# A fused attention and two-layer kernel: three of four key casts on ScalarE instead of two, and the written-out order of the program recomputed

## The chip, the core and the metric

The kernel runs on one core of a Trainium2 chip. A core has engines that each work through a program of their own, in order: TensorE (PE, with its weight loads listed as PEld), VectorE (DVE), ScalarE (ACT), GpSimd (POOL), and SyncE (SP), which issues transfers. The metric is device time in microseconds (us) of one execution, as the median over repeated executions.

## The reference

The inputs are q, k and v of shape (4, 8, 768, 64) (batch, heads, positions, head size), one decay number per head, and two weight matrices, 512x2048 and 2048x512.

```python
# per head, in blocks of 64 positions
intra = (q_b @ k_b.T) * Dmask          # lam^(i-j) on and below the diagonal, 0 above
out_b = intra @ v_b + (q_b * lam_pow) @ kv_state
kv_state = lam**64 * kv_state + (k_b * rev_pow).T @ v_b
# then, on x = all heads side by side, 3072 x 512
h = x @ w_in
g = where(h >= 1, h, where(h <= -1, 0, (h + 1)**2 / 4))
return g @ w_out                        # 3072 x 512, float32
```

## The kernel before, in words

**Tiles.** The 3072 positions are cut into 24 chunks of 128 (C), six to a batch. Attention goes chunk by chunk; four chunks make one of six tiles of 512 positions (MS), on which the two weight layers run. Matrix products take bfloat16 and add up in float32. The decay is put into tables: q is multiplied by a table of lam powers, v by its inverse, so that the mask that is left is only the triangle of ones (`causal`).

**Attention of a chunk.** Chunks 0 to 3 (PLAIN) go a different way, with transposes on PE. Chunks 4 to 23 go as follows, and these are the ones that the change touches. k, q and v of the chunk arrive by three transfers of 256 KB (tiles x1f, x0f and x2f). k is cast to bfloat16 in four pieces, each for half of the partitions and every second head (`f_ki`, lines 259 to 264); the list `KE` says for each piece whether ACT (line 262) or DVE (line 264) does it. The pieces and the scaled q (`f_qn`, line 267, DVE) go to one tile kq, of which there are three. SP then issues one transposing transfer of kq into the tile xq (line 273). POOL scales and casts v in four pieces (line 281) and copies them in two (line 284). PE multiplies k and v into the state pu (line 312), ACT casts the state to ubd (line 315), PE multiplies xq with xq into the scores ps (line 324), DVE multiplies these with the triangle into sc (line 331, "the mask product"), and PE multiplies state and scores into po (lines 349 and 351). ACT casts po to the tile xT (line 358).

**The two layers.** PE multiplies xT with w_in into ph (line 368); there are two ph buffers. ACT takes each to r with a relu and a bias of 1 (line 376). For each two r, DVE makes t (line 382), w (line 386) and gT (line 401), which together are the function g. PE multiplies gT with w_out into py (line 407), ACT copies py to osb (line 412), and SP sends it out (line 416). We call a *block* either one filling of ph (16 matmuls of 128 columns, or 8 of 256) or four matmuls into py. There are 96 of each kind, 192 in all.

**What sets the order.** The order of every engine's program is written out when the program is built. Each operation is entered with `add`: a name, an engine, an assumed length in ns, the operations it needs, and a due time. `run_plan` goes through an imagined time with these lengths; whenever an engine is free it takes, of the operations that are ready, the one due first. What comes out is only the sequence of each engine; on the chip each engine follows its sequence and waits for what it needs. So another assumed length can change the sequence anywhere behind it, on all engines. Where the imagined PE would be idle early on, `run_plan` puts in matmuls on zeros (line 232), and their number follows from the imagined times too. The due time of a piece of k or q is 16000 ns ahead of that of the chunk's po (`due=od - 16000`).

Of the kernel before, what the change touches and what calls it, by code (L numbers as in the profile page):

```python
# [15 lines left out]
def _bc(ap, idx, n):  # L16

    a = list(ap.ap)
    a = a[:idx] + [[0, n]] + a[idx:]
    return bass.AP(ap.tensor, ap.offset, a)  # L20
# [3 lines left out]
def kernel(  # L24
# [29 lines left out]
    CPS = MS // C  # L54

    PLAIN, KA = 4, 1
    LD, RING, VBN, VCN = 6, 6, 620, 600
    KE = ('ACT', 'DVE', 'ACT', 'DVE')
    RW, NR = 2, 3
    DBG = False  # L60

# [2 lines left out]
    ld = ctx.enter_context(tc.tile_pool(name="ld", bufs=LD))  # L64
# [81 lines left out]
    def tabq(i, hp):  # L146
        r = row[:, i * C:(i + 2) * C].rearrange("p (a b) -> p a b", b=C)
        nc.scalar.activation(out=tab_q[:, i:i + 2, hp, :], in_=r, func=AF.Exp, scale=ln_t[:, hp:hp + 1])
# [26 lines left out]
    def add(key, eng, ns, fn, needs=(), due=None, extra=0):  # L175
        OPS[key] = Op(key, eng, ns, fn, needs, due, extra)
        ops.append(OPS[key])
# [60 lines left out]
    def mm(*cols):  # L238
        return sum(c / 2.4 + 3 for c in cols)
# [9 lines left out]
    def cast(c, x, e):  # L249
        t = (ks, qs)[1 - x][c] = qkp.tile([128, H, D], BF16, name=f"c{x}", tag=f"c{x}")  # L250
        if e == "ACT":
            nc.scalar.copy(out=t, in_=qkv_ld[c, x])
        else:
            nc.vector.tensor_tensor(t, qkv_ld[c, x], qkv_ld[c, x], op=AX.max)

    def quarter(t, g, hi):
        return t[HD[g]].rearrange("p (a b) d -> p a b d", b=2)[:, :, hi, :]

    def f_ki(c, g, hi):
        o, i = kq[c % NKQ][HD[hi], HP * g:HP * g + HP, HD[hi]], quarter(qkv_ld[c, 1], g, hi)  # L260
        if KE[2 * g + hi] == "ACT":
            nc.scalar.copy(out=o, in_=i)  # L262
        else:
            nc.vector.tensor_tensor(o, i, i, op=AX.max)  # L264

    def f_qn(c):
        nc.vector.tensor_tensor(kq[c % NKQ][:, 2 * HP:, :].rearrange("p a (b d) -> p (a b) d", b=2), qkv_ld[c, 0],  # L267
                                _bc(tab_n[:, c % NCB, :], 2, D), op=AX.mult)
# [6 lines left out]
    def cast_v(c, g=None, hi=None):  # L275
        tab = tab_k[:, c % NCB, :]
        if c < PLAIN:
            nc.gpsimd.tensor_tensor(vn[c % NV], qkv_ld[c, 2], _bc(tab, 2, D), op=AX.mult)
        else:
            tab = tab[HD[g]].rearrange("p (a b) -> p a b", b=2)[:, :, hi]  # L280
            nc.gpsimd.tensor_tensor(vn[c % NV][HD[hi], HP * g:HP * g + HP, :], quarter(qkv_ld[c, 2], g, hi), _bc(tab, 2, D), op=AX.mult)  # L281

    def f_vb(c, hi):
        nc.gpsimd.tensor_copy(vi[c % NV][HD[hi], :, HD[hi]], vn[c % NV][HD[hi]])  # L284

    def f_t(c):
        ptt[c] = pp_t.tile([128, 2, HP, 128], BF16, name="pt", tag="pt")
        for i, x in enumerate((ks, qs)):
            for hp in range(HP):
                nc.tensor.transpose(out=ptt[c][:, i, hp, :], in_=pair(x[c], hp), identity=ident)  # L290

    def f_kb(c):
        kT[c] = ktp.tile([128, HP, 128], BF16, name="kT", tag="kT")
        (nc.scalar.copy if c < KA else nc.vector.tensor_copy)(out=kT[c], in_=ptt[c][:, 0])

    def f_qT(c):
        qT[c] = qtp.tile([128, HP, 128], BF16, name="qT", tag="qT")
        nc.vector.tensor_tensor(qT[c], ptt[c][:, 1], tab_q[:, c % NCB], op=AX.mult)
# [141 lines left out]
    def o_due(c):  # L440
        s, i = c // CPS, c % CPS
        w = CPS // PARTS[s]
        return l_due[1, s, 0, i // w] - LEAD - (w - 1 - i % w) * 8 * STEP
# [46 lines left out]
    for c in range(NCH):  # L490
        od, cb = o_due(c), c % NCB
        P = c < PLAIN
        lu = ("u", c - 1, 1) if cb else ("u", c - 2, 1) if c < PLAIN + 1 else ("u", c - 1, 0)
        lub = [("ub", lu[1], lu[2], hi) for hi in range(2)]
        for x in (1, 0) if P else ():
            e = "DVE" if c == 0 else "ACT"
            add(("cast", c, x), e, 690 if e == "DVE" else 615, lambda c=c, x=x, e=e: cast(c, x, e),
                [("ld", c, x), ("t", c - 3), ("u", c - 3, 1), ("cast", c - 1, x)])
        for hp in range(HP) if P and c % 2 == 0 else ():
            add(("tab", c, hp), "ACT", 410, lambda c=c, hp=hp: tabq(c, hp), [("tab", c, hp - 1), (None, ("kb", 0), ("x", 1))[c // 2]])  # L500
        free = [("xt", c - NKQ), ("u", c - NKQ, 0), ("u", c - NKQ, 1), ("zk", c % NKQ)]
        if not P:
            for g in range(2):
                for hi in range(2):
                    add(("ki", c, g, hi), KE[2 * g + hi], 375, lambda c=c, g=g, hi=hi: f_ki(c, g, hi), [("ld", c, 1)] + free, due=od - 16000)
            add(("qn", c), "DVE", 690, lambda c=c: f_qn(c), [("ld", c, 0), ("tabn",)] + free, due=od - 16000)
        fv = [("ld", c, 2), ("tabk",), ("o", c - NV), ("u", c - NV, 0), ("u", c - NV, 1), ("vb", c - NV, 0), ("vb", c - NV, 1)]
        if P:
            add(("cast", c, 2), "POOL", 1060, lambda c=c: cast_v(c), fv + [("cast", c - 1, 2)], due=-1)
        for g in range(0 if P else 2):  # L510
            for hi in range(2):
                add(("cv", c, g, hi), "POOL", VCN, lambda c=c, g=g, hi=hi: cast_v(c, g, hi), fv + [("cv", c - 1, g, hi)], due=-1)
        for hi in range(0 if P else 2):
            add(("vb", c, hi), "POOL", VBN, lambda c=c, hi=hi: f_vb(c, hi), [("cv", c, 0, hi), ("cv", c, 1, hi), ("o", c - NV), ("zv", c % NV)], due=0)
        if P:
            add(("t", c), "PE", mm(*[128] * 8), lambda c=c: f_t(c), [("cast", c, 0), ("cast", c, 1), ("kb", c - 1), ("qT", c - 1)], due=od - 9000, extra=FILL)
            add(("kb", c), "ACT" if c < KA else "DVE", 590 if c < KA else 430, lambda c=c: f_kb(c), [("t", c), ("s", c - 2, 1)])
            add(("qT", c), "DVE", 690, lambda c=c: f_qT(c), [("t", c), ("o", c - 3), ("qT", c - 1)] + [("tab", c // 2 * 2, hp) for hp in range(HP) if c < NCB])
        else:
            add(("xt", c), "SP", 1800, lambda c=c: f_xt(c), [("ki", c, 0, 0), ("ki", c, 0, 1), ("ki", c, 1, 0), ("ki", c, 1, 1), ("qn", c), ("s", c - NXT, 1), ("o", c - NXT)], due=-0.7, extra=4700)  # L520
        for j in range(1 if P else 0, 2):
            if (cb, j) == (NCB - 1, 1):
                continue
            add(("u", c, j), "PE", mm(*[128 if c < NCB else 64] * 4), lambda c=c, j=j: f_u(c, j),
                [("cast", c, 1), ("cast", c, 2), *(("ki", c, j, hi) for hi in range(2)), *(("cv", c, j, hi) for hi in range(2)), *([("vb", c, 0), ("vb", c, 1)] if c < NCB else []),
                 *([lu] + lub if j == 0 or P else [("u", c, 0), ("ub", c, 0, 0), ("ub", c, 0, 1)])], due=od - 6000 + 1500 * j, extra=FILL)
            for hi in range(2):
                add(("ub", c, j, hi), "ACT", 372, lambda c=c, j=j, hi=hi: f_ub(c, j, hi), [("u", c, j), ("o", (2 * c + j - NUB + 1) // 2)])
        for h in range(0 if P else 1, 2):
            add(("s", c, h), "PE", mm(*[128] * 4) if P else mm(*[64] * 8), lambda c=c, h=h: f_s(c, h),  # L530
                [("kb", c), ("qT", c), ("xt", c), ("m", c, 0) if h and P else ("m", c - 1, 1)],
                due=od - 5500 + 2000 * h, extra=FILL)
            add(("m", c, h), "DVE", 690, lambda c=c, h=h: f_m(c, h), [("s", c, h), ("o", c - 2), ("m", c, 0) if h else None])
        ub = [("ub", c - 1, 1, hi) for hi in range(2) if cb] + [("ub", c, 0, hi) for hi in range(0 if P else 2)]
        add(("o", c), "PE", mm(*[128] * (4 if cb else 0), *[128] * 4) if P else mm(*[64] * (16 if cb else 12)), lambda c=c: f_o(c),
            [("m", c, 1), ("vb", c, 0), ("vb", c, 1), *ub, ("x", c - 1), ("o", c - 1)], due=od, extra=FILL)
        add(("x", c), "ACT", 600, lambda c=c: f_x(c), [("o", c), ("x", c - 1), ("l1", (c // CPS - 2) * FO + FO - 1)])

    n_of = {x: n for n, x in enumerate(l1_order)}
    for n1, (s, i, p) in enumerate(l1_order):  # L540
# [4 lines left out]
            due=l_due[1, s, i, p], extra=FILL)  # L545
# [47 lines left out]
```

## Time and profile before

| | |
|---|---|
| median of 13 executions | 228.55 us (226.49 to 231.53) |
| the profiled execution's own time | 227.48 us |
| its span on the core | 225.3 us |
| clock granted to PE | full throughout |
| busy: PE, DVE, ACT, POOL | 207.7, 175.4, 141.9, 126.7 us |

The profile is of one execution. Its span is 2.2 us shorter than that execution's time, and that execution is 1.07 us under the median. "Busy" is time in which an engine has an instruction running; waits are given with the instruction that ended them. In lists of instructions a row reads: line, engine, operation, tile written <- tiles read, shapes, count, then busy us and mean ns, then idle time of the engine just before.

### The profile page before, as it was taken

The numbers are of one execution on the slowest core, as the hardware profiler recorded it, in microseconds if no ns is written. First come the engines' busy times: TensorE is split into PE (matmuls) and PEld (weight loads), VectorE is DVE, ScalarE is ACT, GpSimd is POOL, SyncE is SP. The second block draws the span as 40 slices with busy tenths as digits, with TensorE's granted clock in tenths as the row PEclk, the third lists the DMA queues.
The fourth block names the chain that finished last, engine by engine and source line by source line (L and its number), as shares of the span: only waits on it lengthen the run. The fifth ranks groups of instructions, "written<-read, shape, count | busy, mean of one in ns | idle before, by whom it ended". The sixth has DMA issues, their size and how long they took to land.

```text
span 225.3 us, 5683 instructions
## 1 busy us (share of the span) xinstructions
PE 207.7 (92%) x2312; PEld 146.9 (65%) x2312; DVE 175.4 (78%) x257; ACT 141.9 (63%) x286; POOL 126.7 (56%) x160
## 2 busy tenths in 40 slices
PE   7799999799799996799997989996999999999993
PEld 3457897466487685587865867765677776766441
DVE  6535899999989999999999799799989555454300
ACT  6757565486396784669756876875568664555121
POOL 8989964599799997926576547556826000000000
PEclk9999999999999999999999999999999999999999
DMA  5999999999999998299987589699374521110212
GB/s 139 220 249 258 258 207 175 254 231 268 272 248 205 258 209 198 67 226 199 204 209 164 137 171 232 152 170 220 90 169 118 54 65 47 49 47 7 89 50 89
DMA packets 98729, 37.59 MB, mean 167 GB/s; under 512 B 90512, under 2 KB 94608, under 8 KB 98704
## 3 DMA queue, kind: packets, MB, share of 16 engines
q1 hardware_dynamic: 93056, 28.84, 58.7%
q0 software_dynamic: 5504, 8.39, 17.4%
q8 instruction: 18, 0.29, 0.6%
q14 instruction: 7, 0.06, 0.1%
q10 hardware_dynamic: 144, 0.00, 0.0%
HBM read 27.27 MB, written 6.29 MB: 149 GB/s over the span
## 4 chain that ended last, share of the span: by engine, by line
PE 52%; DVE 33%; DMA 5%; issue 4%; POOL 3%; ACT 1%; ACTq 0%; POOLq 0%
PE py L407 23%; PE ph L368 23%; DVE kq L264 8%; DVE w L386 7%; DVE t L382 5%; DVE gT L401 5%; DVE kq L267 4%; DVE sc L331 4%; DMA w_in_sb<-in_moe_w_in_dram 3%; DMA x2f<-in_v_dram 2%; PE po L351 2%; PE pu L312 1%; PE po L349 1%; POOL x2f L450 1%; PE ps L324 1%
## 5 line engine op out<-in xcount | busy, mean ns | idle before, releaser
L368 PE MATMUL ph<-xT,w_in_sb 128*128 128x128 bf16 (+1 forms) x1152 | 98.8, 237 | 0.4 <-DMA w_in_sb<-in_moe_w_in_dram 0.4
L407 PE MATMUL py<-w_out_sb,gT 128*128 128x512 bf16 x384 | 94.0, 379 | 0.0
L376 ACT ACTIVATE r<-ph,one 128x512 bf16<-128x512 f32 x96 | 65.5, 687 | 41.4 <-PE ph L368 31.4
L368 PEld LDWEIGHTS <-w_in_sb 128*128 128x128 bf16 x1152 | 80.8, 98 | 13.4 <-DMA w_in_sb<-in_moe_w_in_dram 0.7
L281 POOL TENSOR_TENSOR vn<-x2f,tab_k 64x256 bf16<-64x256 f32 x80 | 65.2, 814 | 42.4 <-DMA x2f<-in_v_dram 34.7
L407 PEld LDWEIGHTS <-gT 128*128 128x128 bf16 x384 | 35.0, 98 | 29.7
L382 DVE TENSOR_SCALAR t<-r 128x1024 bf16<-128x1024 bf16 x48 | 27.2, 567 | 18.0 <-ACT r L376 17.8
L401 DVE TENSOR_TENSOR gT<-w,t 128x1024 bf16<-128x1024 bf16 x48 | 39.8, 829 | 1.5
L386 DVE TENSOR_TENSOR w<-r,t 128x1024 bf16<-128x1024 bf16 x48 | 39.4, 821 | 1.3
L284 POOL COPY vi<-vn 64x512 bf16<-64x512 bf16 x40 | 33.7, 842 | 2.1
L315 ACT CAST ubd<-pu 64x256 bf16<-64x256 f32 x80 | 29.1, 364 | 5.9 <-PE po L349 3.3
L264 DVE TENSOR_TENSOR kq<-x1f 64x256 bf16<-64x256 f32 x40 | 27.2, 680 | 1.0
L358 ACT CAST xT<-po 128x512 bf16<-128x512 f32 x24 | 14.0, 585 | 15.0 <-PE po L351 12.7
L412 ACT COPY osb<-py 128x512 f32<-128x512 f32 x24 | 14.0, 584 | 14.0 <-PE py L407 12.6
L351 PE MATMUL po<-sc,vi 128*128 128x64 bf16 x160 | 11.7, 193 | 10.8 <-DVE sc L331 10.8
L349 PEld LDWEIGHTS <-ubd 128*128 128x128 bf16 x148 | 10.1, 98 | 13.3 <-issue 11.7
L267 DVE TENSOR_TENSOR kq<-x0f,tab_n 128x512 bf16<-128x512 f32 x20 | 18.0, 902 | 0.3
L262 ACT CAST kq<-x1f 64x256 bf16<-64x256 f32 x40 | 16.1, 402 | 0.4
L331 DVE TENSOR_TENSOR sc<-ps,causal 128x512 bf16<-128x512 f32 x20 | 13.7, 685 | 2.1 <-PE ps L324 1.9
L232 PE MATMUL py<-idle 128*128 128x512 bf16 x40 | 12.2, 438 | 1.2 <-DVE one L119 1.2
L349 PE MATMUL po<-xq,ubd 128*128 128x64 bf16 x148 | 12.6, 193 | 0.0
L351 PEld LDWEIGHTS <-vi 128*128 128x128 bf16 x160 | 10.4, 98 | 1.8
(57 smaller groups left out, 110.0 us busy)
## 6 DMA issues: line engine op xcount, KB each, us to landing
out_dram<-osb SPq DMA_DIRECT2D x24, 256.0 KB, 2.5
x1f<-in_k_dram SPq DMA_DIRECT2D x19, 256.0 KB, 3.9
x0f<-in_q_dram SPq DMA_DIRECT2D x19, 256.0 KB, 4.3
x2f<-in_v_dram SPq DMA_DIRECT2D x18, 256.0 KB, 4.1
w_in_sb<-in_moe_w_in_dram POOLq DMA_DIRECT2D x4, 512.0 KB, 8.7
w_out_sb<-in_moe_w_out_dram POOLq DMA_DIRECT2D x4, 512.0 KB, 9.8
x2f<-in_v_dram POOLq DMA_DIRECT2D x6, 256.0 KB, 6.2
x1f<-in_k_dram POOLq DMA_DIRECT2D x5, 256.0 KB, 7.8
```

What stands on the lines that cost most here:

```text
L264: nc.vector.tensor_tensor(o, i, i, op=AX.max)
L267: nc.vector.tensor_tensor(kq[c % NKQ][:, 2 * HP:, :].rearrange("p a (b d) -> p (a b) d", b=2), qkv_ld[c, 0], _bc(tab_n[:, c % NCB, :], 2, ...
L281: nc.gpsimd.tensor_tensor(vn[c % NV][HD[hi], HP * g:HP * g + HP, :], quarter(qkv_ld[c, 2], g, hi), _bc(tab, 2, D), op=AX.mult)
L284: nc.gpsimd.tensor_copy(vi[c % NV][HD[hi], :, HD[hi]], vn[c % NV][HD[hi]])
L315: nc.scalar.copy(out=ubd[(2 * c + j) % NUB][HD[hi], :, HD[hi]], in_=pu[0][HD[hi], :, HD[hi] if c < NCB else HD[0]])
L351: nc.tensor.matmul(po[:, hp, HD[j]], lhsT=vi[c % NV][:, HP * j + hp, :], rhs=sc_sb[c, 1][:, hp, HD[j]], start=(cb == 0 and j == 0), stop=True)
L368: nc.tensor.matmul(ph[:, j * m:(j + 1) * m], lhsT=w_in_sb[:, ko, (i + j) * 128:(i + j + 1) * 128], rhs=xT[s][:, ko, p * m:(p + 1) * m], st ...
L376: nc.scalar.activation(out=r_t[grp][:, i, :], in_=ph_t[s, ni, part], func=AF.Relu, bias=one[:, 0:1])
L382: nc.vector.tensor_scalar(t_t[grp], r_t[grp], 0.5, 1.0, op0=AX.mult, op1=AX.min)
L386: nc.vector.tensor_tensor(w_t[grp], r_t[grp], t_t[grp], op=AX.subtract)
L401: nc.vector.tensor_tensor(o, w, t, op=AX.mult)
L407: nc.tensor.matmul(py_t[s, ms], lhsT=gT[s][:, ko, ms * 128:(ms + 1) * 128], rhs=w_out_sb[:, ko, :], start=(ko == 0), stop=(ko == FO - 1))
```

## The change: three pieces of k on ScalarE, and other assumed lengths

```diff
-    LD, RING, VBN, VCN = 6, 6, 620, 600
-    KE = ('ACT', 'DVE', 'ACT', 'DVE')
+    LD, RING, VBN, VCN = 6, 6, 740, 730
+    KE = ('ACT', 'ACT', 'ACT', 'DVE')
...
-                    add(("ki", c, g, hi), KE[2 * g + hi], 375, lambda c=c, g=g, hi=hi: f_ki(c, g, hi), [("ld", c, 1)] + free, due=od - 16000)
-            add(("qn", c), "DVE", 690, lambda c=c: f_qn(c), [("ld", c, 0), ("tabn",)] + free, due=od - 16000)
+                    add(("ki", c, g, hi), KE[2 * g + hi], 401 if KE[2 * g + hi] == "ACT" else 540, lambda c=c, g=g, hi=hi: f_ki(c, g, hi), [("ld", c, 1)] + free, due=od - 16000)
+            add(("qn", c), "DVE", 750, lambda c=c: f_qn(c), [("ld", c, 0), ("tabn",)] + free, due=od - 16000)
```

The second piece of each of the 20 chunks 4 to 23 goes from line 264 to line 262. Five assumed lengths change: the pieces of k (375 to 401 on ACT and 540 on DVE), the scaled q (690 to 750), and POOL's two kinds of work on v (600 to 730 and 620 to 740). The operations are otherwise the same, except that PE's program has 42 matmuls on zeros instead of 40: where one stood just behind the po of chunk 3, three stand now. The sequences differ on all engines from there on. Three places:

DVE, ahead of the first mask product by the triangle `causal` (chunk 4). kq_128 is the kq tile that chunk 5 uses. Before:

```order
L386 TENSOR_TENSOR w_845<-r,t_843 128x1024
L264 TENSOR_TENSOR kq_128<-x1f 64x4x64 x2
L401 TENSOR_TENSOR gT<-w_845,t_843 128x8x128
L331 TENSOR_TENSOR sc<-ps,causal 128x512
L267 TENSOR_TENSOR kq_128<-x0f,tab_n 128x512
L382 TENSOR_SCALAR t_907<-r 128x1024
```

Now:

```order
L386 TENSOR_TENSOR w_849<-r,t_829 128x1024
L264 TENSOR_TENSOR kq_128<-x1f 64x4x64
L401 TENSOR_TENSOR gT<-w_849,t_829 128x8x128
L267 TENSOR_TENSOR kq_128<-x0f,tab_n 128x512
L331 TENSOR_TENSOR sc<-ps,causal 128x512
L382 TENSOR_SCALAR t_891<-r 128x1024
```

One piece of k is gone from ahead of the mask product, and the scaled q of chunk 5 has come ahead of it.

DVE, around the mask product of chunk 9; kq_128, kq_126 and kq_127 belong to chunks 11, 12 and 13 here. Before:

```order
L267 TENSOR_TENSOR kq_128<-x0f,tab_n 128x512
L382 TENSOR_SCALAR t_1608<-r 128x1024
L386 TENSOR_TENSOR w_1634<-r,t_1608 128x1024
L401 TENSOR_TENSOR gT<-w_1634,t_1608 128x8x128
L264 TENSOR_TENSOR kq_126<-x1f 64x4x64 x2
L267 TENSOR_TENSOR kq_126<-x0f,tab_n 128x512
L331 TENSOR_TENSOR sc<-ps,causal 128x512
L382 TENSOR_SCALAR t_1712<-r 128x1024
L386 TENSOR_TENSOR w_1717<-r,t_1712 128x1024
L401 TENSOR_TENSOR gT<-w_1717,t_1712 128x8x128
L264 TENSOR_TENSOR kq_127<-x1f 64x4x64 x2
```

Now:

```order
L267 TENSOR_TENSOR kq_128<-x0f,tab_n 128x512
L382 TENSOR_SCALAR t_1551<-r 128x1024
L386 TENSOR_TENSOR w_1564<-r,t_1551 128x1024
L401 TENSOR_TENSOR gT<-w_1564,t_1551 128x8x128
L382 TENSOR_SCALAR t_1629<-r 128x1024
L264 TENSOR_TENSOR kq_126<-x1f 64x4x64
L267 TENSOR_TENSOR kq_126<-x0f,tab_n 128x512
L331 TENSOR_TENSOR sc<-ps,causal 128x512
L386 TENSOR_TENSOR w_1692<-r,t_1629 128x1024
L401 TENSOR_TENSOR gT<-w_1692,t_1629 128x8x128
L264 TENSOR_TENSOR kq_127<-x1f 64x4x64
```

Ahead of the mask product one piece of k is gone and the next pair's t has come in its place.

ACT, at the pieces of k of chunks 6 and 7 (kq_126 and kq_127). Before:

```order
L262 CAST kq_126<-x1f 64x4x64 x2
L315 CAST ubd_135<-pu 64x4x64 x2
L376 ACTIVATE r<-ph,one 128x512 x2
L262 CAST kq_127<-x1f 64x4x64 x2
L376 ACTIVATE r<-ph,one 128x512
L315 CAST ubd_133<-pu 64x4x64 x2
```

Now:

```order
L262 CAST kq_126<-x1f 64x4x64 x3
L376 ACTIVATE r<-ph,one 128x512
L412 COPY osb<-py 128x512
L315 CAST ubd_135<-pu 64x4x64 x2
L262 CAST kq_127<-x1f 64x4x64 x3
L376 ACTIVATE r<-ph,one 128x512
```

Three pieces now stand in a row ahead of an r, where two stood.

## The prediction

> **What bounds the kernel now.** The page comes first: who is busy, and what the chain that ended last consists of.
>
> ```profile
> span 225.3 us, 5683 instructions
> PE 207.7 (92%) x2312; PEld 146.9 (65%) x2312; DVE 175.4 (78%) x257; ACT 141.9 (63%) x286; POOL 126.7 (56%) x160
> PE 52%; DVE 33%; DMA 5%; issue 4%; POOL 3%; ACT 1%; ACTq 0%; POOLq 0%
> ```
>
> PE is busy most, yet a third of the chain is DVE. So there are stretches with different limits; the busy times by stretch and the end of the chain show where they part.
>
> ```profile
> core 0: us, PE busy (x) PEld busy (x) DVE busy (x) ACT busy (x) POOL busy (x), PEclk, DMA share, GB/s
> 30.00:157.00 127.00, 116.22 (x1511) 87.83 (x1509) 120.64 (x164) 88.45 (x183) 89.78 (x110) 1.00 0.97 204
> 157.00:226.00 69.00, 64.49 (x518) 41.46 (x514) 36.08 (x56) 33.67 (x61) 10.24 (x12) 1.00 0.27 71
> ...
> 166.32 0.86 PE py L407 x4
> 167.19 0.87 PE ph L368 x8
> 207.68 13.83 PE py L407 x64
> ```
>
> From 157 us on PE works without a gap (the last 4 us are the last output's way out). So every us by which PE gets to that point sooner comes off the total. From 30 to 157 us PE stands 127.00 - 116.22 = 10.8 us, and DVE is busy 95% of the time. The waits of PE in that stretch have one row:
>
> ```profile
> PE po L351 <- DVE sc L331: 10.8, 10, 1.7
> ```
>
> All of PE's standing is ten waits for the mask product. One of the longest, in the timeline:
>
> ```profile
> 85.47 0.87 DVE L264 TENSOR_TENSOR kq<-x1f 64x256 bf16<-64x256 f32 x2
> 86.38 0.99 DVE L267 TENSOR_TENSOR kq<-x0f,tab_n 128x512 bf16<-128x512 f32 x1
> 87.29 0.68 DVE L331 TENSOR_TENSOR sc<-ps,causal 128x512 bf16<-128x512 f32 x1
> 88.02 0.19 PE L351 MATMUL po<-sc,vi 128*128 128x64 bf16 x1 [1.72 <-DVE sc L331]
> ```
>
> This is chunk 9. The mask product is not late because its scores are late; it stands behind two pieces of k and a scaled q in DVE's sequence. That is the work of which the change takes half away. **10.8 us is therefore the most that the change can give.**
>
> **What the change removes and adds.** The prices:
>
> ```profile
> L264 DVE TENSOR_TENSOR kq<-x1f x40: 419/726/806, 30.1 to 170.0; 64x256 bf16<-64x256 f32 x40
> L262 ACT CAST kq<-x1f x40: 390/403/407, 29.6 to 172.1; 64x256 bf16<-64x256 f32 x40
> L401 DVE TENSOR_TENSOR gT<-w,t 128x1024 bf16<-128x1024 bf16 x31 | 27.2, 876 | 1.0
> L386 DVE TENSOR_TENSOR w<-r,t 128x1024 bf16<-128x1024 bf16 x31 | 26.7, 861 | 0.9
> L264 DVE TENSOR_TENSOR kq<-x1f 64x256 bf16<-64x256 f32 x36 | 24.6, 682 | 0.9
> L382 DVE TENSOR_SCALAR t<-r 128x1024 bf16<-128x1024 bf16 x31 | 19.3, 621 | 2.0 <-ACT r L376 1.9
> L267 DVE TENSOR_TENSOR kq<-x0f,tab_n 128x512 bf16<-128x512 f32 x18 | 16.3, 903 | 0.3
> L331 DVE TENSOR_TENSOR sc<-ps,causal 128x512 bf16<-128x512 f32 x16 | 10.9, 684 | 1.3 <-PE ps L324 1.1
> ```
>
> (First two rows: ns of one, least, median and most. The others: from 30 to 157 us.) A piece costs DVE 0.68 us on average, and ACT 0.40. DVE's vary twofold and ACT's hardly. The Trainium skill, "SBUF — State Buffer", section "Who interferes with whom", says that a VectorE instruction with two SBUF inputs contends with GpSimd's reads while ScalarE waits for nobody; this spread agrees with that, and by the short end of 0.42 us the 16 pieces counted below would take 6.7 us off DVE instead of 10.9.
>
> I count, in the sequences, what lies between the mask products of chunks 4 and 19, the first and the last that PE waits for:
>
> ```profile
> 44.89 0.19 PE L351 MATMUL po<-sc,vi 128*128 128x64 bf16 x1 [1.45 <-DVE sc L331]
> 156.58 0.19 PE L351 MATMUL po<-sc,vi 128*128 128x64 bf16 x1 [1.71 <-DVE sc L331]
> ...
> 44.16:88.02 43.86, 39.63 (x532) 29.33 (x532) 41.96 (x54) 30.00 (x63) 38.66 (x48) 1.00 1.12 244
> 88.02:156.58 68.56, 62.73 (x793) 48.06 (x793) 64.58 (x91) 50.15 (x104) 42.80 (x52) 1.00 0.83 179
> ```
>
> *DVE before*: 26 triples t, w, gT at 0.621 + 0.861 + 0.876 = 2.358 us make 61.3; 32 pieces 21.8; 16 scaled q 14.4; 15 mask products 10.3; together 107.8 of 111.7 us. *Now*: the same triples and mask products, 16 pieces 10.9, 15 scaled q 13.5; together 96.0.
>
> *PE before*: 100 blocks. A block is 0.86 to 0.87 us by the rows of the chain, 0.875 with its small gaps, so 87.5; the stretch holds 111.7 less 9.3 of waits (10.8 less the first, 1.45), and the remaining 14.9 are attention, 1.0 a chunk. *Now*: 101 blocks and 15 chunks, 103.4 us. **DVE falls from about equal to PE to 7 us below it**, so most waits should go. Not all, as the sum hides three things:
>
> *Chunk 4.* Up to its mask product DVE's sequence has two pieces less and one scaled q more: -1.36 + 0.90 = -0.46 us. PE has two matmuls on zeros more on the way, 2 x 13.83/64 = 0.43 us, which eat into this same wait. 1.45 - 0.46 - 0.43 = 0.6 us stay. The 0.43 us themselves are PE time that was not there: -0.4 from the gain.
>
> *Chunks 4 to 9.* Here DVE gets 7 triples, 7 pieces, 7 scaled q and 5 mask products, 31.0 us by the same prices, and PE 39 blocks and 5 chunks, 39.1. Much room: 0.3 us left of the 3.5 (43.13 us less 39.6 busy).
>
> *Chunks 9 to 19.* DVE 19 triples, 9 pieces, 8 scaled q, 10 mask products: 65.0 us. PE 62 blocks and 10 chunks: 64.3. Before, by the same count, DVE 68.7 and PE 63.4, and 5.8 us of waits in 68.56. The lead that DVE gains up to chunk 9 can't be kept, since a mask product can't be made ahead of its scores. Lower bound of what stays: 65.0 - 64.3 = 0.7. Upper bound: all 5.8. Nearer to the lower one, since 65.0 is already the sum of overlapping durations (64.58 busy where they add up to 68.7), but DVE must also wait for ACT's r now and then: I take 2.5.
>
> *ACT* gets 20 x 0.40 = 8.0 us more, 16 of them between 30 and 157 us: 88.45 + 6.4 = 94.9 of then some 120 us, 79%. PE waits for none of ACT's work now; I cost this at nothing, covered by ACT's idle time ahead of r:
>
> ```profile
> L376 ACT ACTIVATE r<-ph,one 128x512 bf16<-128x512 f32 x61 | 41.4, 687 | 18.6 <-PE ph L368 10.4 <-issue 2.3 <-DVE w L386 1.8
> L262 ACT CAST kq<-x1f 64x256 bf16<-64x256 f32 x35 | 14.1, 402 | 0.4
> ```
>
> If that cover goes, it is the last rival below. *POOL* and *SP* issue the same work and transfers; POOL's longer assumed lengths move only two of its copies behind the next chunk's casts, and SP issues the transposing transfer of chunk 5 ahead of a load that stood before it.
>
> Sum: 10.8 - (0.6 + 0.3 + 2.5) - 0.4 = **7.0 us**. Against the profiled execution that is 227.48 - 7.0 = 220.5; against the median, 1.07 us above it, **228.55 - 7.0 = 221.5**. Its own range: with 0.7 left between chunks 9 and 19 and nothing before, 9.7 us, 218.9; with all of 5.8 and of 1.45 left, 10.8 - 5.8 - 1.45 - 0.4 = 3.1 us, 225.4.
>
> **The rivals.**
>
> *Inputs take over (gain of about 3).* PE comes to the next wait sooner and finds v or xq not there. For it, in chunk 5:
>
> ```profile
> 41.43 3.28 POOL L281 TENSOR_TENSOR vn<-x2f,tab_k 64x256 bf16<-64x256 f32 x4 [5.28 <-DMA x2f<-in_v_dram]
> 44.77 1.89 POOL L284 COPY vi<-vn 64x512 bf16<-64x512 bf16 x2
> 47.95 0.39 PE L312 MATMUL pu<-vi,kq 128*128 128x128 bf16 x4
> ...
> POOL vn L281 <- DMA x2f<-in_v_dram: 34.7, 12, 5.7
> PEld L324 <- DMA xq<-kq: 0.4, 1, 0.4
> DMA to landing us min/median/max: 3.2/4.2/8.9
> ```
>
> v lands at 41.4, POOL ends at 46.66, PE needs it at 47.95: 1.3 us of room, and the new sequence puts one more block, 0.9 us, ahead of it. Against it: PE was held by such a transfer for 0.4 us in all, and the loads are called for by the pace of the program, so they come sooner too. If about four of the later chunks each lose 1 us to a 4.2 us transposition, 4 of the 7.0 go: 225.5.
>
> *DVE's time is filled again (no change).* The sequence is drawn up with 540 ns for a piece that takes 680, and 750 for a scaled q of 903; the new order may again set mask products behind other work. Chunk 9 shows it: a piece (0.68) is gone from ahead of the mask product, and a t (0.62) has come. If that holds at all ten places, -0.06 us each, the time stays at about 228. Against it: DVE's sum falls all the same.
>
> *ACT holds up r (slower).* Three pieces in a row, 3 x 0.40 = 1.2 us, now stand ahead of an r in ACT's sequence. They wait for k and for a free kq tile, and r waits behind them; there are two ph buffers, so PE stops at the next filling, and DVE's t comes late too. The point from which this decides is 7.0/20 = 0.35 us of PE's time a chunk, less than one piece. At 0.5 us a chunk it costs 10 us: 221.5 + 10 = 231.5. Against it: ACT waited 0.4 us in all ahead of such pieces, and two blocks into py or ph (1.7 us) usually stand between one filling and the need of its buffer. A page speaks for this rival: the Trainium skill, "ScalarE: Activation LUTs", section "Rules for kernel authors", gives simple elementwise work to VectorE, up to about three times faster per element in bf16. The rows here, 390 to 407 ns against 419 at best, are against it; at three times 0.42 ACT would get 25 us instead of 8.0.
>
> **How the numbers follow.** Chances: the forecast 0.63, inputs 0.16, filled again 0.09, ACT 0.12. The measurement tells about 0.5%, 1.1 us, from no change. Faster holds the forecast, the inputs and a little of the third: 0.80. Same: 0.08; slower: 0.12. The range reaches from somewhat below 218.9, as executions of the kernel before differ by 5 us among themselves, over the inputs case to the edge of no change: 218.0 to 227.6, which leaves out ACT's case and most of the third.
>
> **What would show it.** Right: PE's waits for the mask product fall from 10.8 to 2 to 5 us, and PE's last unbroken stretch begins around 150 us; DVE's busy time falls by some 13 us (20 x 0.68), and line 262 has 60 pieces of 0.40. The inputs case: PE or PEld rows that wait for xq or for POOL, over 3 us. Filled again: the waits for line 331 still near 10. ACT: PE's line 368 waiting for r at line 376. Wrong altogether would be a DVE that is less busy and a PE that stands as long as before.

## The result and the profile after

The changed kernel takes 225.23 us (median of 11 executions, 222.28 to 228.88). The kernel before, over 48 executions, takes 228.96 us; each experiment below has executions of the kernel before of its own, on the same chip. The ratio is 0.980 [0.976, 0.984], which is 4.6 us off. A second measurement (experiment 6) gave 0.975 [0.970, 0.980], 5.7 us off. Executions more than 1.5% above the fastest of their kernel in the same measurement are left out of the ratios, here and below, but stand in the medians, so that a difference of medians (3.7 us here) can be smaller than the ratio says.

The profiled execution took 224.76 us, against 227.48 before. The page of the changed kernel, with the groups of the pieces of k:

```profile
span 222.5 us, 5696 instructions
PE 207.7 (93%) x2314; PEld 146.6 (66%) x2314; DVE 161.5 (73%) x237; ACT 149.9 (67%) x306; POOL 126.6 (57%) x160
PE 60%; DMA 17%; DVE 14%; POOL 5%; issue 2%; ACT 1%; POOLq 0%; ACTq 0%; SPq 0%
L262 ACT CAST kq<-x1f 64x256 bf16<-64x256 f32 x60 | 24.1, 402 | 7.0 <-DMA x1f<-in_k_dram 3.5
L264 DVE TENSOR_TENSOR kq<-x1f 64x256 bf16<-64x256 f32 x20 | 12.4, 619 | 7.1 <-DMA x1f<-in_k_dram 4.8
```

DVE is busy 13.9 us less and ACT 8.0 us more; PE's work is the same 207.7 us. In the chain DVE's share fell from 33% to 14%, and the share of DMA rose from 5% to 17%. And pieces of k, on both engines, now have idle time ahead of them that ends when k's load lands. So the limit has moved, and the table of PE's waits says where to:

```profile
PE po L351 <- DVE sc L331: 3.7, 5, 1.3
PE ps L324 <- DMA xq<-kq: 3.1, 3, 1.9
PE ph L368 <- DMA w_in_sb<-in_moe_w_in_dram: 1.5, 2, 1.0
```

(us in total, times, the longest.) PE stands 222.5 - 207.7 = 14.8 us in all, where it stood 17.6. The mask product took 10.8 of that and takes 3.7: -7.1. But PE now stands 3.1 us for xq, where it stood for none (only a weight load was held, once, for 0.4). The wait for w_in is 1.1 us longer; it falls into the start, ahead of the first moved piece, and experiment 6 has it at 0.7 for the same kernel, so it varies between executions. -7.1 + 3.1 + 1.1 + 0.1 of all others = -2.8 us, which is the difference of the two spans. These two executions are thus closer to each other than the ratio, 4.6 us, says of all.

The stretches by their busy times (columns as in the prediction): from 30 to 157 us, then from the mask product's matmul in chunk 4 to that of chunk 9, and from there to that of chunk 19.

```profile
30.00:157.00 127.00, 119.98 (x1542) 89.98 (x1542) 110.58 (x150) 97.74 (x205) 89.72 (x110) 1.00 0.95 206
44.40:86.17 41.77, 40.38 (x525) 28.99 (x524) 32.45 (x43) 31.96 (x69) 35.10 (x45) 1.00 1.09 235
86.17:154.71 68.54, 63.69 (x811) 48.82 (x810) 62.17 (x83) 54.45 (x115) 47.88 (x57) 1.00 0.82 192
```

PE now works 119.98 us of the 127, where it worked 116.22, and DVE 110.58 instead of 120.64. PE's standing in the two stretches by chunk is 1.39 and 4.85 us. Chunk 9, which the prediction showed, in the timeline of the changed kernel:

```profile
82.24 0.77 DVE L382 TENSOR_SCALAR t<-r 128x1024 bf16<-128x1024 bf16 x1 [0.56 <-ACT r L376]
83.06 0.70 DVE L264 TENSOR_TENSOR kq<-x1f 64x256 bf16<-64x256 f32 x1
83.80 0.99 DVE L267 TENSOR_TENSOR kq<-x0f,tab_n 128x512 bf16<-128x512 f32 x1
84.71 0.68 DVE L331 TENSOR_TENSOR sc<-ps,causal 128x512 bf16<-128x512 f32 x1
86.20 0.19 PE L351 MATMUL po<-sc,vi 128*128 128x64 bf16 x1
```

And two rows of its chain of waits:

```profile
155.30 0.87 PE ph L368 x8
156.17 0.86 PE py L407 x4
```

The sequence around chunk 9 is still t, piece, scaled q, mask product, as the prediction's third case feared. But DVE now even has time to wait for r (0.56 us), the mask product ends 0.8 us ahead of PE's need, and PE waits for nothing there. By the chain PE works without a gap from 155 us on, where it did from 157; the prediction had given about 150 as its sign.

The three waits for xq in the timeline of the changed kernel, on the weight loads ahead of the scores, with two of the transfers they waited for:

```profile
32.41 3.10 SPq L273 DMA_TRANSPOSE xq<-kq  x1
43.26 0.29 PEld L324 LDWEIGHTS <-xq 128*128 128x128 bf16 x8 [1.27 <-DMA xq<-kq]
60.80 0.29 PEld L324 LDWEIGHTS <-xq 128*128 128x128 bf16 x8 [0.90 <-DMA xq<-kq]
82.30 2.90 SPq L273 DMA_TRANSPOSE xq<-kq  x1
88.74 0.29 PEld L324 LDWEIGHTS <-xq 128*128 128x128 bf16 x8 [2.06 <-DMA xq<-kq]
```

And the landing times of all 20, from the view of the tile:

```profile
DMA to landing us min/median/max: 3.2/4.6/10.8
```

They are chunks 4, 6 and 10. Chunk 4's transposition was issued at 32.41 us and landed 10.8 us later, though the fastest of the 20 took 3.2. Of the 4.23 us that these weight loads wait, PE stands 3.1: 0.78 us at chunk 4, 0.41 at chunk 6 and 1.94 at chunk 10. For comparison, chunk 4's weight load and chunk 10's transposition in the kernel before:

```profile
41.27 0.29 PEld L324 LDWEIGHTS <-xq 128*128 128x128 bf16 x8 [0.43 <-DMA xq<-kq]
78.54 3.62 SPq L273 DMA_TRANSPOSE xq<-kq  x1
```

So chunk 4's xq now came 2.0 us later, and chunk 10's transposition was issued 3.8 us later, though the kernel as a whole is quicker.

### The profile page after: what moved, and what is told of

It is laid out like the page before. It is cut to its first block, busy times and chain, and to the rows that moved or that the text cites. A ratio compares the mean times of both kernels' runs of the same rounds, so it can differ in the third digit from the quotient of the medians.

```text
span 222.5 us, 5696 instructions
## 1 busy us (share of the span) xinstructions
PE 207.7 (93%) x2314; PEld 146.6 (66%) x2314; DVE 161.5 (73%) x237; ACT 149.9 (67%) x306; POOL 126.6 (57%) x160
## 4 chain that ended last, share of the span: by engine, by line
PE 60%; DMA 17%; DVE 14%; POOL 5%; issue 2%; ACT 1%; POOLq 0%; ACTq 0%; SPq 0%
PE py L407 27%; PE ph L368 25%; DMA xq<-kq 5%; DMA w_out_sb<-in_moe_w_out_dram 5%; DMA w_in_sb<-in_moe_w_in_dram 4%; DVE gT L401 4%; DVE t L382 3%; DVE w L386 2%; DMA x2f<-in_v_dram 2%; DVE sc L331 2%; DVE kq L267 2%; PE po L351 2%; DMA x1f<-in_k_dram 2%; DVE kq L264 1%; PE pu L312 1%
## 5 line engine op out<-in xcount | busy, mean ns | idle before, releaser
L368 PE MATMUL ph<-xT,w_in_sb 128*128 128x128 bf16 (+1 forms) x1152 | 97.5, 237 | 1.5 <-DMA w_in_sb<-in_moe_w_in_dram 1.5
L401 DVE TENSOR_TENSOR gT<-w,t 128x1024 bf16<-128x1024 bf16 x48 | 40.9, 853 | 1.5
L386 DVE TENSOR_TENSOR w<-r,t 128x1024 bf16<-128x1024 bf16 x48 | 38.7, 807 | 1.3
L284 POOL COPY vi<-vn 64x512 bf16<-64x512 bf16 x40 | 33.2, 830 | 2.2
L262 ACT CAST kq<-x1f 64x256 bf16<-64x256 f32 x60 | 24.1, 402 | 7.0 <-DMA x1f<-in_k_dram 3.5
L267 DVE TENSOR_TENSOR kq<-x0f,tab_n 128x512 bf16<-128x512 f32 x20 | 18.5, 927 | 0.8 <-DMA x0f<-in_q_dram 0.5
L264 DVE TENSOR_TENSOR kq<-x1f 64x256 bf16<-64x256 f32 x20 | 12.4, 619 | 7.1 <-DMA x1f<-in_k_dram 4.8
L349 PE MATMUL po<-xq,ubd 128*128 128x64 bf16 x148 | 11.7, 193 | 0.0
```

The costliest lines, as they stand in the source:

```text
L368: nc.tensor.matmul(ph[:, j * m:(j + 1) * m], lhsT=w_in_sb[:, ko, (i + j) * 128:(i + j + 1) * 128], rhs=xT[s][:, ko, p * m:(p + 1) * m], st ...
L386: nc.vector.tensor_tensor(w_t[grp], r_t[grp], t_t[grp], op=AX.subtract)
L401: nc.vector.tensor_tensor(o, w, t, op=AX.mult)
```

## The experiments

The change does two things at once: it takes 20 pieces from DVE, and it recomputes all sequences with new lengths. The main theory (L in the expectations) is that DVE's load decides; its rivals are that the new order does it, that the order is worth nothing either way (N), and that ACT's three pieces in a row cost something. A list `KR` was put beside `KE` in most experiments: `run_plan` draws the sequences up from `KE`, and `KR` says which engine really gets the piece. In the old order with `KR` changed, no engine's sequence differs but for the pieces that go from the one to the other.

### 1 and 5: the pieces moved, the order left

```diff
-    KE = ('ACT', 'DVE', 'ACT', 'DVE')
+    KE, KR = ('ACT', 'DVE', 'ACT', 'DVE'), ('ACT', 'ACT', 'ACT', 'DVE')
...
-        if KE[2 * g + hi] == "ACT":
+        if KR[2 * g + hi] == "ACT":
```

> The sequence of every engine is the one of before; only the engine on which the second piece of k runs is changed, so that DVE loses 20 pieces and ACT gets 20, at the same places. Theory L (the gain is DVE's load): PE's wait for the mask product falls from 10.8 us to 5 or less and the time by 1.5 to 2.5%, ratio 0.975 to 0.985, as with the whole change. Theory O (the gain is the new order): the waits stay above 8 us and the ratio is 0.992 or more. If ACT's place for the piece is a bad one (rival ACT), ratio above 1.

Experiment 1 gives no ratio: its executions took 221.37, 227.55, 227.69 and 230.75 us, and only the first could be counted. That one was profiled; its waits of PE:

```profile
PE po L351 <- DVE sc L331: 4.1, 6, 1.6
```

The waits for the mask product fall as with the whole change, and none for xq stands in its table. One execution is no basis for saying that the old order is better or worse, so the same kernel ran again, in five rounds.

> The old order with the second piece of k on ACT, again, for an interval. If the full-clock time of 221.4 us of its first look holds: ratio 0.970 to 0.978, more gain than the whole change, so the recomputed order gives part of it back (theory G, given back by the order). If that look was a lucky one: ratio 0.978 to 0.985, as the whole change (theory N, the order does nothing either way).

Ratio 0.978 [0.974, 0.983], median 223.94 us. Its waits:

```profile
PE po L351 <- DVE sc L331: 3.4, 4, 1.6
PE ps L324 <- DMA xq<-kq: 2.2, 2, 1.3
PE ph L368 <- ACT r L376: 1.1, 2, 0.8
```

The waits for xq are there this time, and two for r. The move alone gives what the change gives; the 221.4 us of the first time was the low end of its spread.

### 2: the order alone

```diff
-    KE = ('ACT', 'DVE', 'ACT', 'DVE')
+    KE, KR = ('ACT', 'ACT', 'ACT', 'DVE'), ('ACT', 'DVE', 'ACT', 'DVE')
```

with the change's five lengths, so that the sequences are those of the change, and two pieces of each chunk on DVE.

> The sequences of the changed kernel, but two pieces of k on DVE as before. Theory L: DVE is as loaded as before, the mask products come late in a sequence that was drawn up for less DVE work, PE's wait for them is 10 us or more, ratio 0.995 to 1.015. Theory O: the ratio is below 0.99.

Ratio 1.002 [0.997, 1.006]. DVE is busy 173.0 us, and PE waits as before:

```profile
PE po L351 <- DVE sc L331: 10.0, 7, 2.8
```

The recomputed order by itself, with two pieces on DVE, gives nothing that can be measured.

### 3 and 4: half of the source change each

Experiment 3 has the new `KE` with the old lengths, experiment 4 the new lengths with the old `KE`; both recompute the order.

```diff
# experiment 3
-    KE = ('ACT', 'DVE', 'ACT', 'DVE')
+    KE = ('ACT', 'ACT', 'ACT', 'DVE')
# experiment 4
-    LD, RING, VBN, VCN = 6, 6, 620, 600
+    LD, RING, VBN, VCN = 6, 6, 740, 730
...  and 401 / 540 / 750 for the pieces and the scaled q
```

> The list KE of the change with the old assumed lengths, and the order that follows from these. Theory L: DVE busy falls by about 14 us as with the whole change, ratio 0.975 to 0.99. Theory O (the truer lengths make the order): ratio 0.99 or more.

> The new assumed lengths with the old list KE, two pieces on each engine, and the order that follows. Theory L: DVE stays at about 175 us busy and the ratio between 0.99 and 1.01. Theory O: a good part of the gain, ratio 0.99 or less.

Experiment 3: 0.977 [0.967, 0.987], with DVE busy 163.7 us and the first row below. Experiment 4: 1.010 [0.996, 1.025], with DVE busy 175.8 us and the second.

```profile
PE po L351 <- DVE sc L331: 6.6, 8, 1.4
```

```profile
PE po L351 <- DVE sc L331: 9.5, 8, 2.0
```

With the old lengths PE still waits 6.6 us for mask products, 2.9 more than with the change, and yet the time is within the error of the change's: in that execution no wait for xq stands beside it. Whether it is the better lengths that remove these 2.9 us, and whether the waits for xq then take their place, isn't shown: there is one profile of each, and the waits for xq come and go between executions (experiments 1 and 5).

### 6 and 7: the change again, and without most loads of q

Experiment 6 is the change as it is, beside experiments 5, 7 and 8 on one chip.

> The changed kernel itself, on the same chip as the old order with the moved piece. Theory G: ratio 0.978 to 0.988, one per cent or more above that of the old order; PE waits for xq and DVE and ACT wait for loads of k, some 3 us of PE's time. Theory N: the two ratios are within 0.5% of each other.

Ratio 0.975 [0.970, 0.980]. Its waits:

```profile
PE ps L324 <- DMA xq<-kq: 3.3, 3, 1.9
PE po L351 <- DVE sc L331: 2.4, 4, 0.9
```

The ratio is within 0.003 of experiment 5's, as theory N has it. Again 3.3 us for xq, in three waits: both profiles of the changed kernel have them. With the old order they came in experiment 5 and not in experiment 1, so how much of them there is changes from one execution to the next.

Experiment 7 thins out the transfers: 18 of the loads of q are not issued, and the q of an earlier chunk is used.

```diff
+        if x == 0 and c >= SW: return qkv_ld.update({(c, 0): qkv_ld[c - SW, 0]})
```

> The changed kernel, its order kept, without the 18 loads of q from chunk 6 on (the scaled q is made from the q of the chunk six before, so a quarter of the traffic is gone and the output is not the reference's). Theory D (pieces of k and PE wait because transfers queue behind each other): the waits for x1f and xq go from 12.8 and 3.1 us to under a third, the transposition lands in 4.0 us or less in the median, and the time falls by 2 to 4 us against the change. Theory P (the waits come from where the order puts the pieces, whatever the traffic): waits and time as in the change within 1 us.

Ratio 0.973 [0.968, 0.977], not told apart from experiment 6; the 2 to 4 us that theory D expected did not come. Its profiled execution took 227.62 us; the other three, from which the ratio comes, took 222.02 to 224.03. That profile shows:

```profile
L262 ACT CAST kq<-x1f 64x256 bf16<-64x256 f32 x60 | 24.1, 402 | 0.8
L264 DVE TENSOR_TENSOR kq<-x1f 64x256 bf16<-64x256 f32 x20 | 13.1, 654 | 0.6
xq<-kq SPq DMA_TRANSPOSE x20, 3.2
```

(Two groups of instructions, and the transfers with their number and median landing time in us.) And its waits of PE:

```profile
PE ps L324 <- DMA xq<-kq: 6.3, 1, 6.3
```

The 7 us of idle time ahead of the pieces are gone on both engines, the median transposition lands in 3.2 us instead of 4.6, and chunks 6 and 10 wait no more. One wait is left, chunk 4's, and in this execution it was 6.3 us long. (The loads of q are left out from chunk 6 on.) After that wait PE came to the scores of chunks 6 and 10 only at 66.5 and 91.7 us, where with the change it did at 59.9 and 86.7, so that it waits for nothing there proves little. The transpositions of these two chunks did land sooner, at 59.56 and 85.54 us instead of 60.76 and 88.69, which fits theory D. That q's loads cause the waits in chunks 6 and 10 is not shown by this, and chunk 4's wait came without most of them.

### 8, 9 and 11: more and fewer pieces on DVE

Experiments 8 and 9 keep the old order and put none and three of the four pieces of a chunk on DVE. Experiment 11 puts none there and recomputes the order with the new lengths.

```diff
# experiment 8
+    KE, KR = ('ACT', 'DVE', 'ACT', 'DVE'), ('ACT', 'ACT', 'ACT', 'ACT')
# experiment 9
+    KE, KR = ('ACT', 'DVE', 'ACT', 'DVE'), ('ACT', 'DVE', 'DVE', 'DVE')
# experiment 11
+    KE = ('ACT', 'ACT', 'ACT', 'ACT')
```

> The old order with both of DVE's pieces of k on ACT, all four. Theory L (DVE's load): PE's wait for the mask product goes below 2.5 us and the time is 1 to 3 us under that with one piece moved. Rival ACT (ACT now holds up r): PE waits for r or for ubd, and the time is no better or worse than with one piece moved.

> The old order with three pieces of k on DVE and one on ACT: with the runs before it a row of doses in one order (DVE 3, 2, 1, 0 pieces). DVE is already 95% busy from 30 to 157 us, so under theory L each of the 16 pieces in that stretch, 0.68 us, goes on the path: 9 to 12 us more, ratio 1.035 to 1.055, waits for the mask product 18 to 24 us. If DVE's load does not set the time (theory O): ratio below 1.015.

> All four pieces of k on ACT as in the run with both moved, but with the new assumed lengths and an order recomputed for them. If the order is worth nothing either way (theory N): ratio 0.962 to 0.973, as with the old order. If the order drawn up for the load helps: below 0.962. If it puts work ahead of its inputs (theory G): 0.975 or more.

With three, two, one and none on DVE, in the old order:

| pieces on DVE | ratio | step, us |
|---|---|---|
| 3 | 1.037 [1.023, 1.051] | |
| 2 (before) | 1 | 8.5 |
| 1 (experiment 5) | 0.978 [0.974, 0.983] | 5.0 |
| 0 (experiment 8) | 0.967 [0.963, 0.972] | 2.5 |

Steps are differences of the ratios by the median of the kernel before on that chip, 228.74 us for the first and 229.37 for the others. Each step takes 20 pieces, some 13.6 us of work, from DVE. Of that work about 63% lay on the path at first, then 37%, then 18%: by these values, the more of DVE's load is gone, the less the next part is worth. The errors of the steps are about 3.2, 1.0 and 1.5 us, so that only the first and the last step are clearly told apart. Experiment 9's profiled execution took 360.11 us, at a granted clock of 0.563, where the other three took 235.36 to 238.74; the waits that its expectation names are therefore not read. What PE waits for in experiment 8:

```profile
PE ps L324 <- DMA xq<-kq: 1.7, 2, 0.9
PE ph L368 <- ACT r L376: 0.8, 2, 0.6
PE po L351 <- DVE sc L331: 0.8, 1, 0.8
```

and its busy times from 30 to 157 us:

```profile
30.00:157.00 127.00, 122.42 (x1555) 91.64 (x1553) 101.91 (x134) 106.32 (x227) 93.06 (x114) 1.00 0.99 208
```

DVE and ACT now carry about the same, 101.91 and 106.32 us of the 127; mask products cost 0.8 us, and r, with all 80 pieces on ACT, no more than that. **This kernel has the lowest median of those that give the reference's output**: 221.69 us, 7.5 us under the kernel before (0.0327 x 229.37), and 0.008 under experiment 6 on the same chip. That it is faster than the kernel before is shown; that it is faster than the change is likely, as the two intervals overlap a little.

Experiment 11's ratio, 0.989 [0.975, 1.003], is too wide to say whether it is faster than the kernel before. But it lies above experiment 8's, 0.967 [0.963, 0.972], and the intervals don't overlap, so with all pieces on ACT the order does count: the one recomputed with the new lengths is the worse one, by 0.022, some 5 us (theory G's value, not N's). The two were measured on different chips, each against the kernel before. In experiment 11's profiled execution the mask product is no limit any more; the largest rows are transfers:

```profile
PE ps L324 <- DMA xq<-kq: 2.8, 3, 1.9
PE ph L368 <- DMA w_in_sb<-in_moe_w_in_dram: 2.1, 2, 1.4
PE po L351 <- DVE sc L331: 1.0, 4, 0.3
```

### 10: one load of w_out instead of four

Besides k, q and v, the four loads of w_out (512 KB each) share the transfer engines with the transpositions at the start. Here the changed kernel loads one quarter, and all products into py use it. The edit does one thing more: the load of k for chunk 6 is made to wait for the third load of w_out (`GATE` in the kernel), and without that load it goes out sooner.

```diff
+        if i > WS: return w_dma.append(w_dma[WS])
...
-            nc.tensor.matmul(py_t[s, ms], lhsT=gT[s][:, ko, ms * 128:(ms + 1) * 128], rhs=w_out_sb[:, ko, :],
+            nc.tensor.matmul(py_t[s, ms], lhsT=gT[s][:, ko, ms * 128:(ms + 1) * 128], rhs=w_out_sb[:, ko % 4, :],
```

> The changed kernel, its order kept, with only the first of the four 512 KB loads of w_out; all second-layer products use that quarter, so the output is not the reference's. Theory D (the transposition of chunk 4 is slow because it shares the transfer engines with the loads of w_out): xq of chunk 4 lands before 40 us instead of 43, PE's wait for it goes from 1.3 to 0, and with it 0.5 to 2 us of the time against the change, ratio 0.965 to 0.975. If the transposition's own length or its place sets the wait: it lands at 41 us or later as before, time as in the change.

Median 220.89 us, ratio 0.968 [0.959, 0.978]. The transposition for chunk 4, the load of k for chunk 6 and the scores of chunk 4, in the timeline:

```profile
32.09 1.51 SPq L273 DMA_TRANSPOSE xq<-kq  x1
33.70 0.52 SPq L450 DMA_DIRECT2D x1f<-in_k_dram  x1
41.73 0.40 PE L324 MATMUL ps<-xq 128*128 128x64 bf16 x8
```

The landing times of all transpositions, and the first row of PE's waits:

```profile
DMA to landing us min/median/max: 3.2/4.3/7.2
```

```profile
PE po L351 <- DVE sc L331: 4.8, 5, 2.0
```

Issued 0.3 us before that of the change, the transposition now lands in time, after 5.7 us, at 37.79: the scores start at 41.73 without a wait, and in chunks 6 and 10 too no wait for xq is left. There the earlier loads can be the reason as well: k for chunk 6 was called for at 33.70 us instead of 37.15, and those behind it sooner too. All loads of q are there, so the waits of chunks 6 and 10 can vanish with them in place. One execution without these waits would prove little, as experiment 1 had none either. But all four executions took 220.14 to 221.64 us, less than the shortest of the change in either measurement (222.28 and 221.94). The profiled one took 220.88, 3.9 less than the change's, with 3.1 less of waits for xq, 1.1 more for the mask product and the rest in the start. By the ratios the difference to the change is 0.007 to 0.012 (1.5 to 2.6 us), and the intervals overlap. So these loads, with the calls that hang on them, are the likely reason for the missing part of the gain, 1.5 to 2.6 us by the ratios; the 3.9 us are of single executions.

The profiles together say when PE waits for xq. Where chunk 4's transposition landed by 41.8 us (before, 41.23; experiments 1 to 4, 41.21, 40.38, 41.02 and 41.76; experiment 10, 37.79), no row of PE's waits for xq stands in the table. Where it landed at 42.1 us or later (experiments 8 and 5, 42.12 and 42.13; experiment 6, 42.45; experiment 11, 42.92; the change, 43.22; experiment 7, 47.95), PE waits 1.7 to 6.3 us for xq, in experiment 11 in later chunks only. Both orders are on both sides, and so is one and the same kernel (experiments 1 and 5). Experiment 9 is left out.

## Why the prediction was right, and where it was not

**The forecast** was 221.5 us, from 218.0 to 227.6: faster, by 7.0. It is faster, and the time lies in the range, but 3.7 us above the forecast by the first measurement's median; by the ratios the gain is 4.6 and 5.7 us instead of 7.0, and by the two profiled executions 2.8.

**DVE's load as the cause**: shown. The move alone gives 0.978, the order alone 1.002, and the dose from three pieces to none goes one way all along. (By the prediction's own sums DVE was not "about equal to PE" between chunks 4 and 19 before, but 5.4 us above it: 107.8 against 87.5 + 14.9. The 7 us below it now are rightly summed.)

**The waits for the mask product that stay**: 0.6 + 0.3 + 2.5 = 3.4 us predicted, 3.7 measured, and 2.4 in experiment 6. By stretch, with the individual waits: nothing in chunk 4 (0.6 predicted), 0.83 in chunk 6 (0.3), and 0.86, 1.31, 0.28 and 0.46 in chunks 11, 12, 16 and 19, 2.9 together (2.5). That chunk 4 had none is no success: there PE stood for xq instead, one step earlier.

**The prices**: 13.9 us off DVE for 20 x 0.68 = 13.6, and 8.0 on ACT as reckoned. By the short end of 0.42 us it would have been 8.4. What makes a piece long on DVE can be read from the trace of before: the 5 pieces during which POOL ran nothing took 419 to 422 ns, the 14 during which POOL was busy for nine tenths of the time or more took 714 to 806. The contention that the Trainium skill's page "SBUF — State Buffer" describes ("Who interferes with whom") fits this, and also the pieces that stayed, which still take 0.62 us on average. DVE's busy time between chunks 4 and 9 was 32.45 us for a reckoned 31.0, and between 9 and 19 62.17 for 65.0.

**The step that failed** is the one that says of POOL and SP: "issue the same work and transfers", costed at nothing. The transfers were the same, but in the profiled execution they came later and took longer. Their price was 3.1 us (3.3 in experiment 6), by which the gain of the profiled execution falls short, together with the longer start. That is the rival "inputs take over", at the size it was given (over 3 us), and it came on top of the forecast instead of in its place. It did not come as that rival had it, by PE being sooner alone. At chunk 4 PE came later: its work ahead of the scores ended at 42.5 us, before at 41.3. The transposition, issued at 32.4 us both times, took 10.8 us instead of 8.9. There had been no room (the 0.4 us that the prediction quoted were chunk 4's). At chunks 6 and 10 PE came 0.6 and 2.5 us sooner, but xq landed 3.5 and 4.5 us later than before: SP had issued these transpositions 2.0 and 3.8 us later, and they were 1.5 and 0.8 us longer on their way. The prediction argued against the rival that "the loads are called for by the pace of the program, so they come sooner too". In this execution it was the other way round: SP, which works through its list in order, stood at its load of v for chunk 6 until 45.2 us, before until 43.2, and what was behind it came later.

How much of this is the change's own doing is not shown. The median landing went from 4.2 to 4.6 us and the longest from 8.9 to 10.8, but one and the same kernel had 9.1 us for the longest in experiment 1 and 10.6 in experiment 5. With fewer loads of w_out the kernel takes 220.9 us, near the forecast of 221.5, which had no such waits in it; it is another kernel, though, whose mask products still cost 4.8 us.

**The two matmuls on zeros** (-0.4): not told apart; PE's busy time is 207.7 us in both, with a few records missing from any trace.

**"DVE's time is filled again"**: not so. The t that comes ahead of chunk 9's mask product is there, and the mask product is early all the same. The order with the change's sequences and two pieces on DVE waits 10.0 us, with one piece 3.7: load, not order.

**"ACT holds up r"**: not so. In the changed kernel PE waits for no r; with the pieces moved in the old order it waits 1.1 us in all (experiment 5), and with all four on ACT 0.8, some 0.05 a chunk, against the 0.35 from which the rival would have decided. The Trainium skill, "ScalarE: Activation LUTs", section "Rules for kernel authors", which gives simple elementwise work to VectorE, points the wrong way here: the piece is shorter on ACT (402 ns against 619), and DVE was the fuller engine. Its factor of three is for instructions with one source in bf16; DVE's piece here reads float32 through two inputs (line 264).

**Open**: which transfers hold chunk 4's transposition up, and in what order. Experiment 10 makes w_out's loads the likely ones; experiment 7 shows that the wait comes without q's later loads too. Why PE's weight load waited 1.27 us for it in the change's profiled execution and 6.8 in experiment 7's, with fewer transfers, no run here tells, nor why the recomputed order is the worse one with all pieces on ACT.

## What to carry to other kernels

Before a stall is counted as a gain, look at what arrives just ahead of it: an input with no room left can become the next wait, and its landing time under load, which varies from one execution to the next, is its price, not its fastest. The parts of a change that moves work and reorders it can be told apart by running the new placement in the old order and the old placement in the new one; a dose in a fixed order then shows how much of the next step is still on the path. And where one engine of a pair is fuller, the placement of the work counted for far more here than better assumed lengths in the plan, though with the work placed best a recomputed order lost most of the gain.

## What the runs showed of the hardware that was not expected

*A wait can cost more than its length.* In experiment 7's profiled execution PE stood 6.3 us for chunk 4's xq. The stretches from 42 to 46 us, within the wait, and from 46 to 50, in which the scores start:

```profile
42.00:46.00 4.00, 0.00 (x0) 0.00 (x0) 0.69 (x2) 0.20 (x1) 0.17 (x1) 0.93 1.11 132
46.00:50.00 4.00, 2.01 (x12) 1.01 (x13) 1.36 (x2) 0.00 (x0) 3.50 (x6) 0.50 1.19 234
```

The clock granted to PE (the third number from the end) was 0.50 when PE came back; from 50 to 54 us it was 0.71, and 1.00 from there on. So some 4.3 us of PE's work ran at half the clock, which by this estimate cost another 2 us. The Trainium skill, "TensorE: Matmul & The Clock Gate", Part 1, has the clock go to half after an idle window of about 3.4 us, and these rows agree. The waits of the changed kernel itself, 1.9 us at the longest, left it at 1.00.

*A transposition of one kq lands in 3.2 us or in over 10*, with the same bytes: 3.2 the fastest, 4.6 the median, 10.8 the slowest of the change, chunk 4's, while three of the loads of w_out were on their way (they landed at 34.39, 37.13 and 45.97 us). With three of the four left out, chunk 4's took 5.7 and the slowest 7.2.

*DVE's pieces vary with POOL, ACT's do not.* The same cast takes from 0.42 to 0.81 us on DVE, and 0.39 to 0.41 on ACT. On DVE it is 0.42 with POOL idle all along and 0.71 or more with POOL busy for nine tenths of it or more (kernel before); on ACT the pieces of these two kinds took 394 to 404 and 390 to 407 ns.
